# A causal convolution and a routed two-layer network: another order of loads, copies and biases in the head

## The chip, the cores and the metric

The kernel runs on one core of a Trainium2 chip. The metric is device time in microseconds: the median of several executions. One execution was also profiled; its span is the time from the first to the last instruction that the profile shows. The engines are TensorE (PE, with PEld for the weight loads), VectorE (DVE), ScalarE (ACT), GpSimd (POOL) and SyncE (SP, which here only issues DMAs).

## The reference

`x` is 8 x 3584 x 192 in float32. Per head of 24 channels (8 heads) a causal convolution with 7 taps runs along the sequence; the taps are a softmax of `weight`. The rows that come out (28672 of 192) go through a gate, each to one of 8 experts, and through that expert's two layers.

```python
w = softmax(weight)                                  # 8 heads x 7 taps
y = np.einsum('hk,bskhg->bshg', w, x_unf)            # x_unf: the 7 rows up to s
y = y.reshape(N, D)                                  # N = 28672, D = 192
logits = y @ w_gate + modality_bias[modality_id]     # N x 8
e_idx = np.argmax(logits, axis=1)
gate_w = softmax(logits)[np.arange(N), e_idx]
for e in range(E):
    mask = e_idx == e
    h = np.maximum(y[mask] @ w1[e], 0.0)             # 192 -> 1024
    out[mask] = gate_w[mask, None] * (h @ w2[e])     # 1024 -> 192
```

## The kernel before

**The head's unit is a group.** A tile is 112 rows of one batch element. The 256 tiles are dealt out in 19 groups of 4, 4, 8, 8, 8 and then 16 tiles (`QUADS_OF_GROUP`, in quads of four tiles); g0 to g18 below. A block is the same 112 rows of all eight batch elements, 8 tiles; a group of 16 tiles holds two blocks. For each group `Group` does the following, as parts of a generator (`body`) that the main loop advances:

- `load`: x of four tiles per DMA, on SP's queue (384 KB).
- `convolve(h)`: a head is one matmul with a banded matrix, `band` (128 x 112 per head), into a PSUM tile `cv` out of four. Groups below 10 (`WHOLE_X`) multiply in float32, later ones with `band_hi`, `band_lo` and x split in two. The result is copied to the row buffer `y`, by ScalarE for heads with h % 3 < 2 and by VectorE for the others, one copy for each block (L284, L286). There are four `y` buffers (y0 to y3), each for one block; `routed_y` deals them out in turn, one for each block of a group, a group of 4 tiles having one to itself.
- `bias_of`: GpSimd makes the modality bias of the group's tiles in two operations (L293 multiply, L296 add).
- `turn`, `gate`, `logits`, `choose`: a transpose on VectorE, the gate's product, and the argmax with the softmax's denominator. GpSimd writes the row numbers into `y` with an iota (L363).
- `place`: each row's position in its expert's list (`idx`); `send`: one indirect DMA per tile on GpSimd's queue (`scatter`, L212) writes 112 rows into `routed_rows` in HBM.

**The routed steps.** The groups are gathered in chunks; the first chunk has groups 0 to 3 (24 scatters). When a chunk's groups are placed, VectorE makes a table of slots, each a run of rows of one expert. For a slot SP loads w1 (`raw1`, L626 and L628) and w2 (`raw2`, L631), which are split in high and low halves by ScalarE and VectorE (`split`, L100 and L101), and `bring` loads its rows, a lot of two passes of 256 rows at a time: 4 DMAs `near`, 8 DMAs `far` and 1 DMA `tags` (L656). These wait for the chunk's scatters to land. `turn` transposes a pass (`tp`); `first` (L707) and `second` (L727, L731) are the two products in three or two terms, `hh` and `hl` (L710, L711) the halves between them. The finished rows `o` go out by another indirect DMA on GpSimd's queue (L746).

**What sets the order.** Each engine runs its instructions in the order of the program. The main loop (`run`) puts the head's parts between the steps by due times: `marks` and `due` say how many parts are to stand ahead of which step. `AHEAD` parts stand ahead of the first step, `WAIT` empty ones ahead of the last scatters of the first chunk. `tc.issue_after` puts one instruction behind another on its engine. In the head, `warm(n)` gives TensorE n matmuls that nothing reads, so that it is not idle. A `y` buffer is written again only when the scatters that read it have landed, so the copies into it wait on them; the two buffers of a group's two blocks are written head by head in turn, first and second block.

**The filler.** A dummy slot behind the routed rows is filled with a constant tile by 8 DMAs on ScalarE's queue (`make_filler`, L594).

## Time and profile before

| | |
|---|---|
| executions | 1268.9, 1269.66 and 1277.72 us, median 1269.66 us |
| the profiled execution | 1275.32 us |
| its span | 1273.5 us |
| mean granted clock of TensorE in it | 0.985 |
| busy: PE, DVE, ACT, POOL | 96%, 78%, 58%, 42% of the span |
| the chain that ended last | PE 80%, DVE 7%, issue 4%, DMA 3%, POOL 2%, SP's queue 2%, ACT 2% |

The profiled execution is 5.66 us above the median. Busy shares are means over the span, and the stages differ: the head, in which groups are made and no routed step runs, ends near 69 us; up to about 900 us parts of groups stand between the routed steps, after it only routed steps. The granted clock is given as a share of full speed, where 1.00 is 2.4 GHz and 0.50 is 1.2 GHz.

### The profile page before, as it was taken

How to read it: one execution, taken by the hardware profiler on the slowest of the kernel's cores; microseconds unless marked ns; L12 is line 12 of the kernel's file. 1: busy time of each engine (PE TensorE's matmuls, PEld its weight loads, DVE VectorE, ACT ScalarE, POOL GpSimd, SP SyncE). 2: the span in 40 equal slices, each digit the busy share in tenths (PEclk: the TensorE clock that was granted, in tenths of full speed). 3: DMA queues.
4: the chain of work that ended last, by engine and by line, in shares of the span. 5: the costliest groups of instructions: out<-in, count | busy, mean ns of one | idle time of the engine just before them, and what ended most of it. 6: DMA issues, size and time to landing. Idle time of an engine off the chain costs nothing.

```text
span 1273.5 us, 28724 instructions
## 1 busy us (share of the span) xinstructions
PE 1223.5 (96%) x9106; PEld 1189.3 (93%) x9106; DVE 999.1 (78%) x2545; ACT 735.6 (58%) x1644; POOL 538.3 (42%) x574
## 2 busy tenths in 40 slices
PE   9668799999999999999999999999999999999996
PEld 7467689999999999999999999999999999999996
DVE  5669788787888788877888788877877676687895
ACT  2245465565665666656565666556555555566774
POOL 4736655353636343443636344343536222121221
PEclk9889899999999999999999999999999999999998
DMA  6678355324355445426444444333326234496441
GB/s 174 193 164 210 100 137 123 94 72 109 75 134 137 108 103 129 104 61 141 97 115 101 107 100 125 88 84 71 73 54 177 54 78 109 102 253 159 113 108 46
DMA packets 317525, 145.91 MB, mean 115 GB/s; under 512 B 229170, under 2 KB 303531, under 8 KB 317364
## 3 DMA queue, kind: packets, MB, share of 16 engines
q1 hardware_dynamic: 291748, 98.64, 36.3%
q0 software_dynamic: 23232, 44.30, 10.9%
q8 instruction: 73, 1.20, 0.4%
q10 hardware_dynamic: 2384, 1.06, 0.3%
q14 instruction: 88, 0.72, 0.2%
HBM read 118.16 MB, written 51.82 MB: 133 GB/s over the span
## 4 chain that ended last, share of the span: by engine, by line
PE 80%; DVE 7%; issue 4%; DMA 3%; POOL 2%; SPq 2%; ACT 2%; DVEq 0%; POOLq 0%; ACTq 0%
PE hps L707 37%; PE po L727 23%; PE po L731 11%; PE cv L279 5%; PE gt L323 3%; DVE hl L711 1%; DMA routed_rows<-y,idx 1%; SPq L656 1%; POOL routed_rows L212 1%; DVE w1b L101 1%; PE hps L115 1%; DMA xr<-in_x_dram 1%; DVE xl L101 1%; DMA x<-in_x_dram 1%; DVE tp L683 1%
## 5 line engine op out<-in xcount | busy, mean ns | idle before, releaser
L727 PE MATMUL po<-w2b,hh 128*128 128x384 f32 x1824 | 556.3, 355 | 3.5 <-DVE o L745 2.2
L707 PE MATMUL hps<-sxh,w1b 128*128 128x256 f32 x1824 | 486.2, 289 | 11.2 <-ACT sxh L692 8.5
L710 ACT ACTIVATE hh<-hps 128x512 fp32r<-128x512 f32 x456 | 272.5, 598 | 312.6 <-PE hps L707 305.9
L711 DVE SCALAR_TENSOR_TENSOR hl<-hps,hh 128x512 fp32r<-128x512 f32 x456 | 311.3, 685 | 179.6 <-ACT hh L710 176.9
L731 PE MATMUL po<-w2b,hl 128*128 128x192 f32 x1824 | 443.3, 253 | 0.0
L212 POOL DMA_INDIRECT routed_rows<-y,idx x256 | 269.1, 1051 | 334.5 <-DVE hl L711 169.5
L746 POOL DMA_INDIRECT out_dram<-o,tags x228 | 239.4, 1050 | 370.8 <-DVE o L745 299.4
L707 PEld LDWEIGHTS hps<-sxh,w1b 128*128 128x128 f32 x1824 | 345.6, 190 | 21.4 <-DVE hl L711 9.5
L707 PE MATMUL hps<-sxs,w1b 128*128 128x256 f32 x1824 | 364.6, 281 | 0.5 <-DVE sxs L694 0.5
L727 PEld LDWEIGHTS po<-w2b,hh 128*128 128x128 f32 x1824 | 344.3, 189 | 5.1 <-DVE o L745 3.3
L731 PEld LDWEIGHTS po<-w2b,hl 128*128 128x128 f32 x1824 | 346.4, 191 | 0.0
L707 PEld LDWEIGHTS hps<-sxs,w1b 128*128 128x128 f32 x1824 | 280.7, 190 | 0.8 <-DVE sxs L694 0.8
L707 PE MATMUL hps<-sxl,w1b 128*128 128x256 f32 x912 | 257.1, 282 | 0.0
L707 PEld LDWEIGHTS hps<-sxl,w1b 128*128 128x128 f32 x912 | 173.4, 190 | 2.2
L101 DVE TENSOR_TENSOR w1b<-raw,w1b 128x512 fp32r<-128x512 f32 x152 | 101.1, 675 | 4.5 <-ACT w1b L100 4.0
L743 ACT ACTIVATE lowp<-po,tags 128x192 f32<-128x192 f32 x228 | 83.5, 418 | 30.8 <-PE po L727 30.8
L284 ACT COPY y<-cv 112x192 f32<-112x192 f32 (+1 forms) x198 | 53.5, 318 | 79.9 <-PE cv L279 54.6
L101 DVE TENSOR_TENSOR w2b<-raw,w2b 128x384 fp32r<-128x384 f32 x152 | 80.9, 542 | 15.2 <-ACT w2b L100 14.9
L100 ACT CAST w1b<-raw 128x512 fp32r<-128x512 f32 x152 | 92.4, 621 | 0.7
L745 DVE SCALAR_TENSOR_TENSOR o<-po,tags,lowp 128x192 f32<-128x192 f32 x228 | 84.4, 411 | 2.3 <-ACT lowp L743 2.3
L692 ACT CAST sxs<-tp 64x128 fp32r<-64x128 f32 x228 | 67.9, 298 | 30.3 <-DVE tp L685 27.5
L100 ACT CAST w2b<-raw 128x384 fp32r<-128x384 f32 x152 | 76.2, 513 | 3.6 <-DMA raw<-in_moe_w_dram 2.5
(133 smaller groups left out, 1028.5 us busy)
## 6 DMA issues: line engine op xcount, KB each, us to landing
raw<-in_moe_w_dram SPq DMA_DIRECT2D x38, 768.0 KB
raw<-in_moe_w_dram SPq DMA_DIRECT2D x38, 512.0 KB
raw<-in_moe_w_dram SPq DMA_DIRECT2D x76, 256.0 KB
xr<-in_x_dram SPq DMA_DIRECT2D x36, 384.0 KB
near<-routed_rows SPq DMA_DIRECT2D x212, 64.0 KB
x<-in_x_dram SPq DMA_DIRECT2D x26, 384.0 KB
far<-routed_rows SPq DMA_DIRECT2D x456, 16.0 KB
routed_rows<-filler SPq DMA_DIRECT2D x8, 776.0 KB
```

The lines of the kernel that those rows point to most:

```text
L100: nc.scalar.copy(out=hi, in_=raw)
L101: return nc.vector.tensor_tensor(out=lo, in0=raw, in1=f(hi), op=ALU.subtract).ins
L212: state["scatter"] = nc.gpsimd.indirect_dma_start(out=scr, out_offset=bass.IndirectOffsetOnAxis(ap=idx, axis=0), in_=src, in_offset=None,).ins
L692: nc.scalar.copy(out=hi, in_=raw)
L707: nc.tensor.matmul(hps[:, u, :], wa[:, c, fs], mv[z], start=n == 0, stop=n == len(terms) - 1)
L710: nc.scalar.activation(out=hh, in_=hps, func=AF.Relu)
L711: hl_ins = nc.vector.scalar_tensor_tensor(out=hl, in0=hps, scalar=0.0, in1=f(hh), op0=ALU.max, op1=ALU.subtract)
L727: nc.tensor.matmul(po, hh[:, u, js], wb[:, c, :], start=c == 0, stop=c == NF - 1, skip_group_check=True)
L731: nc.tensor.matmul(po[:, 0:D], hl[:, u, js], wb[:, c, 0:D], start=False, stop=False, skip_group_check=True)
L743: nc.scalar.activation(out=lowp, in_=po[:, D:2 * D], func=AF.Copy, scale=gate)
L745: turn_behind(nc.vector.scalar_tensor_tensor(out=o, in0=po[:, 0:D], scalar=gate, in1=lowp, op0=ALU.mult, op1=ALU.add))
L746: st = nc.gpsimd.indirect_dma_start(out=out, out_offset=bass.IndirectOffsetOnAxis(ap=tag.bitcast(I32)[:, j, 1:2], axis=0), in_=o, in_offse ...
```

## The change

1. **x loads.** The x of groups 0 to 4 lies in two buffers (`PACKS`) rather than in one each, in turn, and all its loads are issued at the start; those of groups from 2 on wait for the band's DMA (`behind_band`). The filler is one DMA of all its 776 KB on SP's queue, behind them.
2. **Biases.** Those of the first 48 tiles (g0 to g5) are made in one multiplication and one addition (`first_bias`), before any group; later groups make their own, as before.
3. **Convolutions.** Groups below 10 go by block and in pairs of heads (`convolve_pair`): two matmuls of 192 columns into one PSUM tile and one copy of 384 columns to `y`, by VectorE for each fourth part less two, else by ScalarE. The first block's four pairs come first, then the second's. g0 and g1 share one `y` buffer, and a group of 4 tiles takes its half.
4. **Bands.** `band_hi` and `band_lo` are made at group 8 rather than at the start. `mt` is copied behind the gate's copies on VectorE.
5. **Weights.** w2 of the first slot is asked for behind w1, before the row loads.
6. **Rows.** A lot's `far` rows come in 4 DMAs of 32 KB rather than 8 of 16 KB, so 9 loads a lot rather than 13; the rows of a lot are dealt to its two passes in stripes.
7. **TensorE.** `WARM2` = 20 more warm matmuls stand ahead of the first routed step, and the first convolutions of groups 2 to 4 stand behind an earlier group's gate (`GATED`).

```diff
+BEFORE_BAND = 2
+GATED = {2: 1, 3: 1, 4: 2}
+PACKS = (0, 4, 8), (0, 8)
...
-WARM2 = 0
+WARM2 = 20
...
-        nc.sync.dma_start(out=band, in_=bass.AP(lines.tensor, 0, [[1, P], [wide, H], [1, MB]]))
+        state["band"] = nc.sync.dma_start(out=band, in_=bass.AP(lines.tensor, 0, [[1, P], [wide, H], [1, MB]])).ins
...
-        split(hi, lo, band)
...
-        nc.vector.tensor_copy(out=mt.rearrange("p b s -> p (b s)"), in_=mt_ps)
+        with tc.issue_after(state["wg"]):
+            nc.vector.tensor_copy(out=mt.rearrange("p b s -> p (b s)"), in_=mt_ps)
...
-    def routed_y():
-        turns["y"] = turns.get("y", -1) + 1
+    def routed_y(fresh):
+        turns["y"] = turns.get("y", -1) + fresh
...
+    def make_bias(dst, n, ids):
+        nb = ids.shape[1]
+        nc.gpsimd.tensor_tensor(
+            out=dst.rearrange("p (s b) e -> p s b e", s=n), in0=ids.rearrange("p b s -> p s b").unsqueeze(3).broadcast_to([MB, n, nb, E]),
+            in1=step.unsqueeze(1).unsqueeze(1).broadcast_to([MB, n, nb, E]), op=ALU.mult)
+        nc.gpsimd.tensor_tensor(out=dst, in0=dst, in1=start_row.unsqueeze(1).broadcast_to([MB, n * nb, E]), op=ALU.add)
+
+    def behind_band(ins):
+        tc.add_manual_dep(ins, state["band"].name, mybir.DependencyInfo(
+            mybir.DependencyClass.Sync, mybir.DependencyReason.DATA), reason="the bands come first")
...
+            packed = sum(len(p) for p in PACKS)
+            pack = sum(g >= sum(len(p) for p in PACKS[:i]) for i in range(1, len(PACKS))) if g < packed else len(PACKS) + g - packed
+            at = ([i for p in PACKS for i in p] + [0] * NG)[g]
...
-                self.x = xp.tile([P, NT, D], F32, name="x", tag=self.place_x)
+                if at == 0:
+                    turns["x"] = xp.tile([P, NT, D], F32, name="x", tag=self.place_x)
+                self.x = turns["x"][:, at:at + 4 * QUADS_OF_GROUP[g], :]
...
+        def load(self, q, after_band=False):
+
+            with tc.issue_after(state["x"]) if self.g >= sum(len(p) for p in PACKS) else nullcontext():
+                self.load_behind(q, after_band)
...
+            if after_band:
+                behind_band(ld.ins)
...
+        def convolve(self, part):
+
+            if part == 0:
+                self.ys = [routed_y(self.b0 == 0) for _ in range(self.blocks)]
+            if self.whole_x:
+                with tc.issue_after(state["gates", GATED[self.g]]) if self.g in GATED and part == 0 else nullcontext():
+                    self.convolve_pair(part)
+                return
+            h = part
...
+        def convolve_pair(self, part):
+            i, h = divmod(2 * part, H)
+            if i >= self.blocks:
+                return
+            cv = ring(ps_t, 4, [MB, 2, self.nb, G], F32, "cv", "t")
+            for k in range(2):
+                hs = slice((h + k) * G, (h + k + 1) * G)
+                nc.tensor.matmul(cv[:, k], band[:, h + k, :], self.x[:, i * NB:i * NB + self.nb, hs], start=True, stop=True)
+            dst = self.ys[i][0:MB, self.b0:self.b0 + self.nb, OVER + h * G:OVER + (h + 2) * G].rearrange("p b (k c) -> p k b c", k=2)
+            if part % 4 != 2:
+                nc.scalar.copy(out=dst, in_=cv)
+            else:
+                nc.vector.tensor_copy(out=dst, in_=cv)
...
+            if self.g < len(AT_ONCE):
+                self.bt = first_bias[:, AT_ONCE[self.g]:AT_ONCE[self.g] + self.tiles]
+            else:
+                self.bt = rt.tile([MB, NT, E], F32, name="bt")[:, 0:self.tiles]
+                make_bias(self.bt, n, mt[:, self.b0:self.b0 + self.nb, self.block:self.block + n])
...
+        early = []
+        for g in range(sum(len(p) for p in PACKS)):
+            early.append(Group(g, chunk_of[g]))
+            for q in range(early[-1].quads):
+                early[-1].load(q, g >= BEFORE_BAND)
+        with tc.issue_after(state["x"]):
+            ins = nc.sync.dma_start(out=scr[DUMMY:DUMMY + TW, :].rearrange("(j p) w -> p j w", p=P),
+                                    in_=filler.unsqueeze(1).broadcast_to([P, TW // P, W])).ins
+        tc.add_to_no_dep_group("rows0", ins)
+        scatters.append((0, ins.name))
+        cur, ends = early[0], iter(())
...
+            if g == WHOLE_X - 2:
+                split(band_hi, band_lo, band)
...
-        for j in range(TW // P):
-            ins = nc.scalar.dma_start(out=scr[DUMMY + j * P:DUMMY + (j + 1) * P, :], in_=dr).ins
-            tc.add_to_no_dep_group("rows0", ins)
-            scatters.append((0, ins.name))
...
-            if i > 0:
-                load_second()
+            load_second()
...
-            squares = src.rearrange("(k j s t) w -> k j t s w", j=NJ, s=P // Q, t=Q)
-            parts += [(far[j * DB + q * Q:j * DB + (q + 1) * Q, k - k0], squares[k, j, :, :, OVER + P + q * Q:OVER + P + (q + 1) * Q])
-                      for k in range(k0, k1) for j in range(NJ) for q in range(DB // Q)]
+            each = squares.shape[1] // NJ
+            parts += [(far[j * DB + q * Q:j * DB + (q + 1) * Q].rearrange("p k s c -> p (k s) c"),
+                       squares[:, j * each:(j + 1) * each, OVER + P + q * Q:OVER + P + (q + 1) * Q])
+                      for j in range(NJ) for q in range(DB // Q)]
...
-            if self.i == lot == 0:
-                with tc.issue_after(ld):
-                    self.load_second()
...
+    first_bias = const.tile([MB, 6 * NB, E], F32, name="first_bias")
+    make_bias(first_bias, 6, mt[:, :, 0:6])
```

GpSimd's queue between the last scatter of g1 and the scatters of g4, of before (`y_219` is g2's buffer, `y_220` g3's):

```order
L363 IOTA y_219 112x8
L293 TENSOR_TENSOR bt<-mt,step 112x64
L296 TENSOR_TENSOR bt<-bt,both 112x64
L212 DMA routed_rows<-y_219,idx 238592x194 x8
L363 IOTA y_220 112x8
L293 TENSOR_TENSOR bt<-mt,step 112x128 x2
L296 TENSOR_TENSOR bt<-bt,both 112x128 x2
L212 DMA routed_rows<-y_220,idx 238592x194 x8
L363 IOTA y_217 112x8
L212 DMA routed_rows<-y_217,idx 238592x194 x8
```

and of after (`y_218` is g2's, `y_219` g3's, `y_220` g4's):

```order
L405 IOTA y_218 112x8
L215 DMA routed_rows<-y_218,idx 238592x194 x8
L405 IOTA y_219 112x8
L215 DMA routed_rows<-y_219,idx 238592x194 x8
L405 IOTA y_220 112x8
L215 DMA routed_rows<-y_220,idx 238592x194 x8
```

The bias operations between the scatters are gone; what is left between them is the iota.

ScalarE's copies of g7, the group whose buffers are read by g5's scatters, of before (`y1` belongs to the first block, `y2` to the second; the last scatters out of `y2` are the latest):

```order
L284 COPY y1_218<-cv_1696 112x8x24
L284 COPY y2_219<-cv_1696 112x8x24
L284 COPY y1_218<-cv_1700 112x8x24
L284 COPY y2_219<-cv_1700 112x8x24
L100 CAST w2b0_91<-raw2_0_87 128x2x192
L692 CAST sxh_1733<-tp_1730 128x256
L692 CAST sxs_1735<-tp_1730 64x128 x2
L710 ACTIVATE hh_1753<-hps_1742 128x512
L284 COPY y1_218<-cv_1768 112x8x24
L284 COPY y2_219<-cv_1768 112x8x24
```

and of after (here the first block is `y0`, the second `y1`):

```order
L328 COPY y0_217<-cv_1653 112x2x8x24
L328 COPY y0_217<-cv_1657 112x2x8x24
L103 CAST w2b0_91<-raw2_0_87 128x2x192
L737 CAST sxh_1690<-tp_1687 128x256
L737 CAST sxs_1692<-tp_1687 64x128 x2
L755 ACTIVATE hh_1710<-hps_1699 128x512
L328 COPY y0_217<-cv_1725 112x2x8x24
L328 COPY y1_218<-cv_1730 112x2x8x24
L328 COPY y1_218<-cv_1735 112x2x8x24
```

The first copy into the second block's buffer stood second; it is now the eighth row, behind a cast of w2, three casts of rows, one `hh` step and three copies into the first block's buffer.

SP's queue around the first row loads, of before (`raw_0_85` is w1, `raw_0_87` w2 of the first slot):

```order
L656 DMA far<-routed_rows 32x4x32
L656 ISA
L656 DMA far<-routed_rows 32x4x32
L656 ISA
L656 DMA tags<-routed_rows 128x4x2
L631 ISA
L631 DMA raw_0_87<-in_moe_w_dram 128x8x192
```

and of after:

```order
L676 DMA raw_0_85<-in_moe_w_dram 64x1024
L679 ISA
L679 DMA raw_0_87<-in_moe_w_dram 128x8x192
L689 TENSOR_LOAD tab
L689 ISA x2
L704 ISA
L704 DMA near<-routed_rows 32x16x32
```

The request for w2 stood behind the last row load; now it stands ahead of the first, and ahead of the register load that begins the row loads.

## Rows read from the trace of the kernel before

**Rows 1.** Windows by stage: busy time of each engine, granted clock, DMA share.

```profile
core 0: us, PE busy (x) PEld busy (x) DVE busy (x) ACT busy (x) POOL busy (x), PEclk, DMA share, GB/s
60.00:80.00 20.00, 8.60 (x40) 7.07 (x38) 9.47 (x18) 6.37 (x14) 4.75 (x6) 0.74 0.61 147
100.00:120.00 20.00, 16.54 (x114) 14.85 (x115) 18.70 (x40) 11.22 (x24) 13.07 (x12) 1.00 0.84 227
120.00:140.00 20.00, 14.37 (x79) 11.29 (x78) 13.12 (x55) 7.38 (x21) 11.29 (x14) 0.83 0.58 152
300.00:1180.00 880.00, 879.22 (x6740) 875.24 (x6739) 696.03 (x1706) 526.13 (x1154) 360.47 (x366) 1.00 0.46 108
```

**Rows 2.** Timeline of POOL, 26 to 66 us.

```profile
36.99 0.94 POOL L212 DMA_INDIRECT routed_rows<-y,idx  x1 [0.30 <-issue]
...
40.66 0.97 POOL L212 DMA_INDIRECT routed_rows<-y,idx  x1 [1.86 <-issue]
...
50.59 0.81 POOL L293 TENSOR_TENSOR bt<-mt,step 112x128 f32<-112x128 f32 x2
51.36 0.86 POOL L296 TENSOR_TENSOR bt<-bt,both 112x128 f32<-112x128 f32 x2
...
61.13 0.94 POOL L212 DMA_INDIRECT routed_rows<-y,idx  x1 [0.30 <-issue]
```

**Rows 3.** Chain of waits, 60 to 82 us: start, duration, what.

```profile
61.13 2.44 DMA routed_rows<-y,idx
```

**Rows 4.** Waits of the SP queue, 40 to 80 us: total, times, longest, us.

```profile
SPq L656 <- DMA routed_rows<-y,idx: 10.4, 3, 8.0
```

**Rows 5.** Timeline of ACT, 50 to 80 us; idle time before in brackets.

```profile
52.58 0.54 ACT L284 COPY y<-cv 112x192 f32<-112x192 f32 x2 [7.37 <-DMA routed_rows<-y,idx]
...
76.27 1.75 ACT L100 CAST w2b<-raw 128x384 fp32r<-128x384 f32 x4 [2.51 <-DMA raw<-in_moe_w_dram]
```

**Rows 6.** Timeline of ACT around 94 and 133 us.

```profile
94.77 0.76 ACT L284 COPY y<-cv 112x192 f32<-112x192 f32 x3 [1.35 <-DMA routed_rows<-y,idx]
...
133.11 0.76 ACT L284 COPY y<-cv 112x192 f32<-112x192 f32 x3 [8.66 <-DMA routed_rows<-y,idx]
```

**Rows 7.** Timeline of PE, 124 to 145 us.

```profile
133.48 3.68 PE L279 MATMUL cv<-x,band 128*112 128x384 f32 x6 [5.63 <-ACT y L284]
```

**Rows 8.** Chain of waits, 100 to 140 us.

```profile
100.60 2.17 PE cv L279 x6
...
127.47 5.41 DMA routed_rows<-y,idx
...
137.17 1.18 PE hps L707 x10
```

**Rows 9.** Timeline of ACT, 13 to 18 us.

```profile
14.25 0.94 ACT L100 CAST band_hi<-band 128x896 fp32r<-128x896 f32 x1 [6.32 <-DMA band<-tap_lines]
14.25 2.29 ACTq L594 DMA_DIRECT2D routed_rows<-filler  x5
16.59 0.52 ACT L284 COPY y<-cv 112x96 f32<-112x96 f32 x3 [1.41 <-DMA routed_rows<-filler]
```

**Rows 10.** Copies into tile y: duration ns min/median/max, first and last start, forms.

```profile
L284 ACT COPY y<-cv x198: 238/322/357, 16.6 to 895.2; 112x192 f32<-112x192 f32 x186, 112x96 f32<-112x96 f32 x12
L286 DVE COPY y<-cv x66: 257/347/359, 16.6 to 889.9; 112x192 f32<-112x192 f32 x62, 112x96 f32<-112x96 f32 x4
```

**Rows 11.** Timeline of the SP queue, 58 to 78 us.

```profile
66.03 4.38 SPq L656 DMA_DIRECT2D far<-routed_rows  x8
...
71.28 0.40 SPq L631 DMA_DIRECT2D raw<-in_moe_w_dram  x1
```

**Rows 12.** Window of 130 to 135 us, columns as in rows 1.

```profile
130.00:135.00 5.00, 1.52 (x3) 0.86 (x4) 1.30 (x7) 1.86 (x7) 0.99 (x1) 0.50 0.87 283
```

**Rows 13.** Timeline of POOL, 100 to 140 us.

```profile
103.27 0.95 POOL L212 DMA_INDIRECT routed_rows<-y,idx  x1 [7.05 <-ACT y L284]
...
127.47 0.97 POOL L212 DMA_INDIRECT routed_rows<-y,idx  x1 [0.26 <-DVE pos L386]
```

More of the change, by code (lines that the diff above doesn't have):

```diff
@@ L179, in make_gate @@
             nc.vector.tensor_copy(out=whole[rows, :, q * Q:q * Q + E], in_=wg[rows])
-            nc.vector.tensor_copy(out=parts[rows, :, q * Q:q * Q + 2 * E], in_=f(wgs[rows]))
+            state["wg"] = nc.vector.tensor_copy(out=parts[rows, :, q * Q:q * Q + 2 * E], in_=f(wgs[rows])).ins
         return whole, parts
@@ L267, in part @@
             split(self.xh[:, part, :], self.xl[:, part, :], self.xr[q])
-        def convolve(self, h):
-            if h == 0:
-                self.ys = [routed_y() for _ in range(self.blocks)]
+        def convolve(self, part):
[6 more added lines that the diff above has]
+            h = part
             cv = ring(ps_t, 4, [MB, self.tiles, G], F32, "cv", "t")
             hs = slice(h * G, (h + 1) * G)
-            if self.whole_x:
-                terms = ((band, self.x[:, 0:self.tiles, :]),)
-            else:
-                terms = (band_hi, self.xh), (band_hi, self.xl), (band_lo, self.xh)
+            terms = (band_hi, self.xh), (band_hi, self.xl), (band_lo, self.xh)
             for n, (wt, xt) in enumerate(terms):
@@ L397, in send @@
             for t in range(t0, t1):
-                scatter(self.chunk, self.idx[:, t:t + 1], self.ys[t // NB][0:MB, t % NB, :])
+                scatter(self.chunk, self.idx[:, t:t + 1], self.ys[t // NB][0:MB, self.b0 + t % NB, :])
     chunk_of = [c for c, n in enumerate(GROUPS_OF_CHUNK) for _ in range(n)]
     FIRST = GROUPS_OF_CHUNK[0]
+    AT_ONCE = [4 * sum(QUADS_OF_GROUP[:g]) for g in range(NG) if sum(QUADS_OF_GROUP[:g + 1]) <= 12]
     def parts_of(g):
@@ L415, in body @@
     def body(cur, after):
-        if after:
+        if after and not after.xr:
             for q in range(min(3, after.quads)):
@@ L429, in body @@
                 yield
-            if t == 0 and after and after.whole_x and after.quads > 3:
+            if t == 0 and after and after.whole_x and after.quads > 3 and len(after.xr) == 3:
                 after.load(3)
@@ L452, in all_groups @@
     def all_groups():
-        cur, ends = Group(0, 0), iter(())
-        for q in range(cur.quads):
-            cur.load(q)
-            cur.part(q)
+        early = []
[9 more added lines that the diff above has]
+        cur, ends = early[0], iter(())
         for g in range(NG):
-            after = Group(g + 1, chunk_of[g + 1]) if g + 1 < NG else None
+            if g == WHOLE_X - 2:
+                split(band_hi, band_lo, band)
+            after = (early[g + 1:g + 2] or [Group(g + 1, chunk_of[g + 1])])[0] if g + 1 < NG else None
             done, tiles = 0, 4 * QUADS_OF_GROUP[g - 1]
@@ L682, in turn @@
             with tc.issue_after(state["o"]) if "o" in state else nullcontext():
-                nc.vector.transpose(out=tp[:, 0:NJ].rearrange("p j (s t) -> p (j s) t", t=Q),
-                                    in_=self.rows[lot][:, k0 * T // Q:(k0 + 1) * T // Q])
+                nc.vector.transpose(out=tp[:, 0:NJ].rearrange("p j (s t) -> p j s t", t=Q),
+                                    in_=self.rows[lot].rearrange("p (j k s) t -> p j k s t", j=NJ, s=P // Q)[:, :, k0])
                 nc.vector.transpose(out=tp[:, NJ].rearrange("p (s t) -> p s t", t=Q), in_=self.ends[lot][:, k0])
@@ L695, in turn @@
             self.h["x", k] = [z.rearrange("p j s -> p (j s)") for z in (xh, xl, xs)]
[L696 removed]
+            self.h["tag", k] = self.tags[lot].rearrange("p (j k) o -> p j k o", j=NJ)[:, :, k0]
             state["vector"] = turned
```

36 lines of the change are left out of this document (15 added, 21 removed).

## The prediction

> **What bounds the kernel now.** I read the windows by stage first. In the long stretch from 300 to 1180 us TensorE is busy for 879.22 of 880 us at a granted clock of 1.00 [rows 1]. Nothing that the change does to other engines can shorten that stretch, and its amount of TensorE work stays as it is; what is left to win lies in front of it, where TensorE stands idle: 11.4 us between 60 and 80, 3.5 between 100 and 120, 5.6 between 120 and 140 [rows 1]. The last steps after 1240 us wait too, but no edit touches them. Since TensorE never rests after 180 us, each microsecond by which the routed steps start earlier, or by which a stall in the head gets shorter, should come off the end, unless another wait takes its place.
>
> Then I followed what holds the first routed step. The chain is POOL's row of scatters: the first four groups have 24, one every 1.25 us, the last from 61.13 [rows 2], and it lands 2.44 us later [rows 3]; only then may SP ask for the rows, for which its queue has waited 8.0 us [rows 4]. Behind that ScalarE waits 2.51 us more for w2 [rows 5]. Last I looked for the long stall. At 133 us ScalarE has waited 8.66 us for scatters to leave a y buffer [rows 6], TensorE 5.63 us for ScalarE [rows 7], and the chain of waits names the scatter issued at 127.47, which took 5.41 us to land [rows 8].
>
> **The change, part by part.** All sums are made against the profiled execution: 1275.32 us, span 1273.5. That lies 5.66 above the median of the three runs, 1269.66; I carry the same 5.66 off at the end.
>
> *A. Up to the last scatter of the first four groups.* ScalarE issues five filler DMAs at once, 2.29 us long, behind the cast of band_hi; the first eviction starts at 16.59 after 1.41 us of that wait [rows 9]. With the filler on SP and the band split moved to group 8, the eviction can start when the first convolution is there, a little after 14.4: 2.1 us sooner. In groups 0 and 1 a pair of heads leaves PSUM in one copy of 192 columns instead of two of 96. From the fastest copy (96 columns, 0.238) and the median (192 columns, 0.322) [rows 10], three copies at 0.32 take the place of six at 0.24, some 0.5 us in the chain of a group. So the indices of group 2 come 2.6 us sooner. POOL can follow, since between the end of group 1's last scatter (36.99 + 0.94 = 37.93) and the first of group 2 (40.66) it has 2.7 us without a scatter [rows 2]. Between groups 2 and 3 it makes four bias operations, 0.81 and 0.86 us in two pairs, from 50.59 to 52.2 [rows 2]; these go, leaving the iota, so 1.45 us go. Together -4.0. The bound on the small side counts POOL's bias work ahead of group 3 alone: -1.5. The large side lets group 2's scatters follow group 1's with no gap but the iota, all moved by 2.1: -5.9. The one large bias pair of 112x384 at the start has no row; two 112x128 take 0.81 together [rows 2], so I put it at 0.6 to 1.2 us an operation, and it runs while VectorE makes the indices of group 0, for which POOL has to wait. That wait is its cover; without it up to 2.4 us would be late.
>
> *B. w2 sooner.* ScalarE's wait of 2.51 us ahead of w2's cast [rows 5] is for a request issued at 71.28, behind thirteen row loads [rows 11]. It now stands ahead of the row loads, before SP's wait for the scatters, and lands with w1. Of the 2.51 us I take 1.9, because TensorE at its low clock needs part of that time for the first products anyway; bounds 0 and -2.5. Nothing that is late stands behind it on SP's queue: the first row load waits for the scatters for 8.0 us there [rows 4].
>
> Against this stands what a scatter does under load. The last scatter of the first chunk lands in 2.44 us [rows 3], the one at 127.47 in 5.41 [rows 8], while the DMA share rises to 0.87 [rows 12]. If w2 and the x loads that now come earlier were still moving, the first row loads would start 3.0 us later, and A to D would come to 3.0 less. *The Trainium skill* says so on the page "DMA: Bandwidth & Descriptors", section "Latency and other measured facts": an access to HBM takes 0.2 us on average and 2 us at high load, and with a lighter load a DMA's fixed cost falls. By that rule the last scatter would land up to 1.8 us later (an estimate from that page), so that the sum would be smaller by it; the two rows above agree in direction, with a difference of 3.0. I don't take it as likeliest: w2 is requested ahead of that wait of 8.0 us [rows 4], and the request at 71.28 had landed by 76.27 [rows 5, 11], thus in under 5 us.
>
> *C. The y buffers by block.* In before a copy of y1 and a copy of y2 alternate on ScalarE, head by head, so that the first head's second copy needs all scatters of the buffer that is freed last. In after the four pairs of the first block are written first; ScalarE's first row on the second buffer is the eighth of the group's stretch, no longer the second. Until it blocks TensorE, TensorE now has five more pairs of convolutions, at 0.36 (six in 2.17), and two more steps of the routed products, each 2.3 (ten products of the first kind take 1.18, the second kind about as much) [rows 8]: 1.8 + 4.6 = 6.4 us. The stall of 5.63 us [rows 7] lies under that, with little to spare. The copies by ScalarE and the indices of group 6 on VectorE, behind the wait before, are ahead of it now, so POOL's next scatters come sooner too. The granted clock is 0.50 in the five microseconds that follow the stall [rows 12]: six convolutions there take 3.68 us [rows 7], at 100 us they took 2.17 [rows 8], so 1.5 us go with the stall. I take -7.1. Bounds: -2.4 if half the stall stays and the clock still falls in it (2.8, less 0.4 for waits moved elsewhere), -8.7 if all that ScalarE lost, 8.66, comes back. What comes next is POOL: from 103.27 to 127.47 [rows 13] it issues 18 DMAs and a pair of bias operations, 1.34 us to a DMA, and the change leaves them there.
>
> *D. Work on VectorE between 80 and 160.* VectorE is busy 18.70 of 20 us there [rows 1]. A copy of 192 columns costs it 0.347 [rows 10]; of a group of 16 tiles it has some five, after two of 384 columns at an estimated 0.5 (the slope from 96 to 192 columns, 0.09, twice on top). This is 0.87 us a group and three groups lie here: -2.6. The band split, moved in from the head, adds one subtraction of 128x896; ScalarE's cast of that size took 0.94 [rows 9], so I put it at 1.1. With 0.4 for the wait of 1.35 at 94.77 [rows 6]: -1.9, bounds 0 and -4 (no gain at all, or both halves without the split and the wait gone whole).
>
> *E. At nothing.* The pairs cost TensorE the same number of columns, two of 192 for one of 384. The twenty warm matmuls run in idle time between the last head convolutions and the first rows; cover: 8 us and more of idle TensorE, as ScalarE's wait of 7.37 us at 52.58 [rows 5] goes too. They end about 10 us before the first rows, too soon, I think, to hold the clock. Nine row loads instead of thirteen save SP four issues of 0.55 us [rows 11], not on the path, as the first pass needs four near and four far loads either way. x loads behind the band: the band is there when the first convolution starts, and x of group 0 and 1 still goes first.
>
> Sum: -4.0 - 1.9 - 7.1 - 1.9 = -14.9, so 1260.4 for such an execution, 1254.8 for the median.
>
> **The rivals.** *R1, the stall stays.* POOL's stream bounds the second buffer as before: the 18 DMAs at 1.34 us each end just as late against TensorE's work, and ScalarE stands at a later row but as long. For it: POOL has next to no free time from 103.27 to 127.47 [rows 13], and the landing of 5.41 us [rows 8] comes on top. Against: the 6.4 us of new cover. Price: C is lost, -7.8 is left, 1261.9 for the median.
>
> *R2, traffic.* The last scatter of the first chunk lands like the one at 127.47, +3.0 as above: median 1257.8.
>
> *R3, slower.* A far load now holds 32 KB, both passes of a lot. The first pass can't start before all four are there, where before it needed the first four of eight, 2.2 us at 0.55 an issue [rows 11]; if an issue takes time by its bytes, each lot is ready 2.2 us later. It decides if lots come later than their lead: from seven late lots the gain is gone, ten make it +7.1, median 1276.8. Against it: TensorE waits 0.8 us in 880 [rows 1], so lots come with a lead now.
>
> *R4, the warm matmuls hold the clock.* I have put them at nothing; if they reach the first rows, the clock is up there. The granted clock of 60 to 80 is 0.74 [rows 1], and 8.6 us of TensorE work are done there, half of it slow; at full clock 2.2 us go: median 1252.6.
>
> **How the numbers follow.** Forecast as summed 0.52, R1 0.20, R2 0.15, R3 0.05, R4 0.08. The predicted time is that of the forecast, 1254.8. Its own range from the nearer bounds of A to D is 1249 to 1262; the range has to reach R1 with its spread and the far end of R4: 1248 to 1265, leaving out R3, the far tails and some of R1. About one per cent, 1256.96, is what a measurement of this kernel tells from no change. The forecast lies under it by little: 0.33 of its 0.52 is faster, with 0.07 of R4, 0.06 of R2 and 0.03 of R1 0.49; slower is R3 and a tail, 0.06; the rest, 0.45, is within.
>
> **What would show it.** A: the last scatter of the fourth group from about 57 instead of 61.13. B: no wait of ScalarE for w2. C: no idle time of TensorE over 2 us between 110 and 140, and a clock of 1.00 there. D: VectorE's copies of 384 columns at about 0.5. Between 300 and 1180 TensorE busy as now; if it isn't, R3. Wrong would be the prediction by a new wait that I don't see: x of group 5 or 6 late, since x loads now stand behind the band, or a pair's copy that holds a PSUM bank longer than two heads did.

## The result, and the profile after

The changed kernel takes 1260.38 us (median of 6, 1258.32 to 1263.09); the kernel before, run beside it again, 1272.61 (median of 6). The ratio is 0.990, interval 0.9881 to 0.992: 12.2 us less (10.2 to 15.1), against 14.9 forecast. The profiled execution took 1259.42 us with a span of 1257.7, 15.8 less than the span of before; it lies 1.0 under its median, that of before 2.7 over its new one, so the two traces show some 3.7 us more than the medians.

The windows by stage, of after; the columns are those of rows 1.

```profile
60.00:80.00 20.00, 14.27 (x86) 12.97 (x86) 12.69 (x26) 8.78 (x18) 5.70 (x5) 0.76 0.76 153
80.00:100.00 20.00, 18.65 (x133) 17.82 (x134) 19.55 (x50) 13.78 (x31) 7.37 (x9) 1.00 1.00 262
100.00:120.00 20.00, 18.13 (x132) 17.23 (x132) 18.66 (x54) 11.46 (x26) 15.77 (x17) 1.00 0.82 214
120.00:140.00 20.00, 17.34 (x127) 16.44 (x125) 19.36 (x52) 12.17 (x24) 15.57 (x18) 1.00 0.21 64
300.00:1180.00 880.00, 878.73 (x6736) 874.41 (x6735) 698.64 (x1715) 528.81 (x1157) 356.67 (x363) 1.00 0.46 108
```

Nothing moved between 300 and 1180, as forecast. Between 100 and 140 TensorE's idle time fell from 9.1 to 4.5 us, and the granted clock stays at 1.00 there [rows 1]. From 60 to 80 it fell from 11.4 to 5.7.

The way to the first product, of after: POOL from 20 to 60 us, the chain of waits behind its last scatter, SP's queue, then TensorE and ScalarE.

```profile
22.94 1.12 POOL L215 DMA_INDIRECT routed_rows<-y,idx  x1 [5.48 <-DVE ad L418]
...
35.33 0.94 POOL L215 DMA_INDIRECT routed_rows<-y,idx  x1 [2.24 <-DVE lt L372]
...
51.80 2.43 POOL L215 DMA_INDIRECT routed_rows<-y,idx  x1 [0.30 <-issue]
...
55.78 0.94 POOL L215 DMA_INDIRECT routed_rows<-y,idx  x1 [0.30 <-issue]
```

```profile
55.78 2.46 DMA routed_rows<-y,idx
```

```profile
46.75 0.40 SPq L679 DMA_DIRECT2D raw<-in_moe_w_dram  x1
58.45 2.08 SPq L704 DMA_DIRECT2D near<-routed_rows  x4
```

```profile
64.03 0.79 PE L752 MATMUL hps<-sxh,w1b 128*128 128x256 f32 x2 [8.28 <-ACT sxh L737]
```

```profile
13.78 0.66 ACT L328 COPY y<-cv 112x192 f32<-112x192 f32 x2 [6.95 <-PE cv L325]
...
68.61 1.75 ACT L103 CAST w2b<-raw 128x384 fp32r<-128x384 f32 x4
```

The first copy starts at 13.78 instead of 16.59 [rows 9], the scatters of group 2 at 35.33 instead of 40.66, the last of the first chunk at 55.78 instead of 61.13 [rows 2]. It lands in 2.46 us, as before in 2.44 [rows 3], although w2 is asked for at 46.75; the rows are asked for at 58.45, 2.67 us after that scatter's issue. ScalarE casts w2 at 68.61 with no wait, where it waited 2.51 us at 76.27 [rows 5].

How far ahead the changed kernel is at each point can be read from `hh`, which ScalarE makes 456 times, in the same order in both kernels. The first, second, 14th and 22nd, of before and then of after:

```profile
73.17 0.60 ACT L710 ACTIVATE hh<-hps 128x512 fp32r<-128x512 f32 x1 [2.27 <-PE hps L707]
78.67 0.58 ACT L710 ACTIVATE hh<-hps 128x512 fp32r<-128x512 f32 x1
...
122.81 0.59 ACT L710 ACTIVATE hh<-hps 128x512 fp32r<-128x512 f32 x1
...
160.44 0.59 ACT L710 ACTIVATE hh<-hps 128x512 fp32r<-128x512 f32 x1
```

```profile
67.99 0.60 ACT L755 ACTIVATE hh<-hps 128x512 fp32r<-128x512 f32 x1 [2.27 <-PE hps L752]
71.00 0.59 ACT L755 ACTIVATE hh<-hps 128x512 fp32r<-128x512 f32 x1
...
113.75 0.59 ACT L755 ACTIVATE hh<-hps 128x512 fp32r<-128x512 f32 x1
...
144.65 0.59 ACT L755 ACTIVATE hh<-hps 128x512 fp32r<-128x512 f32 x1
```

The lead is 5.2 us at the first, 7.7 at the second (the cast of w2 stands between), 9.1 at the 14th and 15.8 at the 22nd, behind the place of the long stall. It is 17.3 at the 30th and 15.8 in the spans; what moves it there is not settled.

### The profile page after: what moved, and what is told of

It reads as the page before. It is cut to its first block, busy times and chain, and to the rows that moved or that the text cites. A ratio compares the mean times of both kernels' runs of the same rounds, so it can differ in the third digit from the quotient of the medians.

```text
span 1257.7 us, 28099 instructions
## 1 busy us (share of the span) xinstructions
PE 1221.8 (97%) x9206; PEld 1201.2 (96%) x9206; DVE 999.1 (79%) x2530; ACT 732.6 (58%) x1599; POOL 538.9 (43%) x564
## 4 chain that ended last, share of the span: by engine, by line
PE 84%; DVE 7%; DMA 3%; issue 3%; ACT 1%; POOL 1%; SPq 1%; DVEq 0%; POOLq 0%; ACTq 0%
PE hps L752 38%; PE po L772 24%; PE po L776 11%; PE gt L365 4%; PE cv L309 3%; PE cv L325 2%; DVE hl L756 1%; DMA xr<-in_x_dram 1%; PE hps L118 1%; POOL routed_rows L215 1%; DVE w1b L104 1%; DVE xl L104 1%; DVE gx L104 1%; DMA raw<-in_moe_w_dram 1%; ACT lowp L788 1%
## 5 line engine op out<-in xcount | busy, mean ns | idle before, releaser
L739 DVE TENSOR_TENSOR sxs<-tp,sxs 64x128 fp32r<-64x128 f32 x228 | 65.9, 289 | 9.0 <-ACT sxs L737 0.4
```

## The experiments

The first four ran on one chip, beside the kernel before at 1273.33 us; the changed kernel did not run beside them, so they are set against the 0.990 above. The others ran on two more chips, on which the kernel before took 1298.15 us (e12_filler, e3, e11, e5) and 1299.52 us (e13, e12_filler_again, e7, e8). Ratios are to the kernel before on the same chip. On the third chip the changed kernel ran too and comes out at 1.0002; so expectations that name 0.990 don't hold for these, and kernels of one chip are set against each other. "The first chip" below is that of the first four; whether the runs of before and after above were on the same chip isn't known, but the times of before are alike (1272.61 and 1273.33 us).

### The blocks in turn again (e1_alternate)

```diff
-            i, h = divmod(2 * part, H)
-            if i >= self.blocks:
+            part, i = divmod(part, self.blocks)
+            h = 2 * part
+            if h >= H:
                 return
```

> The changed kernel with the pairs of a two-block group written in turn, first block, second block, as before; all else stays. Theory (the order of the blocks hides the wait for the scatters of the later buffer): ScalarE waits 4 to 8 us for scatters again near 120 to 130 us, TensorE stands idle 4 to 6 us behind it at the lower clock, and the time is 5 to 7 us above the changed kernel, about 0.995 of the kernel before. Rival (the stall went because copies are fewer and POOL is earlier, the order matters nothing): no wait of TensorE over 2 us there, 0.990 of the kernel before as the change itself.

Measured: 1269.08 us, 0.9958 (0.9944 to 0.9972), so 0.0058 or 7.4 us above the changed kernel. ScalarE and TensorE of this run, around the stall:

```profile
123.83 0.86 ACT L329 COPY y<-cv 112x384 f32<-112x384 f32 x2 [6.61 <-DMA routed_rows<-y,idx]
```

```profile
124.36 2.90 PE L326 MATMUL cv<-x,band 128*112 128x192 f32 x8 [3.23 <-ACT y L329]
```

```profile
120.00:140.00 20.00, 16.12 (x94) 15.26 (x92) 13.85 (x38) 10.72 (x24) 12.92 (x16) 0.83 0.22 69
```

ScalarE's wait is back with 6.61 us, TensorE's with 3.23, and the clock in the window is 0.83 as before [rows 1]. The window's idle time, 3.9 us, is not all of it; the low clock adds its part, and ScalarE waits in front of copies into `y` for 3.42 us at 87.78 and 3.19 at 157.22 too. Against the changed kernel the 14th `hh` comes 1.4 us later (115.11) and the 22nd 7.0 (151.60). The theory holds in its mechanism, with a shorter wait of TensorE than the 4 to 6 us expected; the rival falls.

### The order of the blocks alone (e10_before_blocks)

In the kernel before, two-block groups in float32 go block by block, two heads to a PSUM tile; copies stay one head wide.

```diff
+            if self.whole_x and self.blocks == 2:
+                i, h = divmod(2 * h, H)
+                cv = ring(ps_t, 4, [MB, 2, self.nb, G], F32, "cv", "t")
+                for k in range(2):
+                    hs = slice((h + k) * G, (h + k + 1) * G)
+                    nc.tensor.matmul(cv[:, k], band[:, h + k, :], self.x[:, i * NB:i * NB + self.nb, hs], start=True, stop=True)
...
+                return
```

> The kernel before with the one edit that two-block groups in float32 are convolved block by block, two heads at a time (copies stay one head wide, as many as before). Theory: the stall at 133 us (TensorE 5.63 idle) goes, and the time falls by some 7 us, 0.9945 of before. Rival (the stall goes only together with the earlier scatters and the fewer copies): it falls by under 2 us, 0.9985 or more.

Measured: 1285.44 us, 1.0085 (1.0064 to 1.0106): 11 us slower. Neither theory said so. TensorE's stall is gone as forecast; its longest waits between 110 and 145 us are 1.2 us, this one and one of 1.18 at 141.35:

```profile
118.17 0.44 PE L739 MATMUL po<-w2b,hh 128*128 128x384 f32 x1 [1.19 <-DVE o L757]
```

But the head is later. VectorE and POOL of this run, at the scatters of group 2:

```profile
43.53 0.36 DVE L282 COPY y<-cv 112x192 f32<-112x192 f32 x1 [3.85 <-DMA routed_rows<-y,idx]
43.80 0.16 DVE L402 CAST idx<-row 112x8 int32<-112x8 f32 x1
```

```profile
44.76 0.97 POOL L212 DMA_INDIRECT routed_rows<-y,idx  x1 [5.67 <-ACT y L280]
```

The copies of group 5's first block go into y1, which group 1's scatters still read; here they stand ahead of the cast of group 2's indices on VectorE, wait there 3.85 us, and group 2's scatters start at 44.76 instead of 40.66 [rows 2]. By `hh` the run is 5.7 us behind the kernel before at the first (78.83) and 9.6 at the 14th (132.41), of which these 4.1 us are a part. From the 14th to the 22nd it takes 32.4 us instead of 37.6: there the order of the blocks gives 5.2 back, as the theory said. The first loss is larger, and some 6 us more are lost later, most of it between 225 and 300 us; why isn't shown. So the order of the blocks takes one wait away and puts another ahead of the first rows, unless the rest of the change (g0 and g1 in one buffer, other buffers for g5, the convolutions behind an earlier gate) keeps it off. Which of these does so wasn't tried.

### w2 behind the row loads again (e2_w2_late)

```diff
-            load_second()
+            if i > 0:
+                load_second()
...
             state["load"] = ld
+            if self.i == lot == 0:
+                with tc.issue_after(ld):
+                    self.load_second()
```

> The changed kernel with the first slot's w2 asked for behind the first lot's row loads again. Theory (w2 was on the path): ScalarE waits some 2 us for it ahead of its cast, and all that follows is 1.9 to 2.5 us later, 0.992 of the kernel before. Rival (VectorE's queue bounds the steps behind it, so w2's moment is hidden): 0.990, as the change.

Measured: 1259.83 us, 0.9881 (0.9858 to 0.9903): no slower than the changed kernel as far as these times can tell. SP's queue and ScalarE of this run:

```profile
61.23 2.32 SPq L705 DMA_DIRECT2D far<-routed_rows  x4
...
64.47 0.39 SPq L679 DMA_DIRECT2D raw<-in_moe_w_dram  x1
```

```profile
69.42 1.75 ACT L103 CAST w2b<-raw 128x384 fp32r<-128x384 f32 x4 [0.34 <-DMA raw<-in_moe_w_dram]
```

The rival on time holds, but not for its reason: the wait itself is nearly gone, 0.34 us, with w2 behind the rows. From the first far load to the request for w2 it is 3.24 us here (61.23 to 64.47); it was 5.25 in before (66.03 to 71.28), where eight far loads took 4.38 [rows 11] and not four 2.32. That loses 0.3 us between the first and the second `hh`, the 0.34 of the wait.

### Filler and band split at the start again (e4_filler_split)

The eight filler DMAs are on ScalarE's queue in `make_filler` again and SP's one is gone; `split(hi, lo, band)` is back in `make_bands`.

```diff
+        split(hi, lo, band)
...
-            if g == WHOLE_X - 2:
-                split(band_hi, band_lo, band)
...
+        for j in range(TW // P):
+            ins = nc.scalar.dma_start(out=scr[DUMMY + j * P:DUMMY + (j + 1) * P, :], in_=dr).ins
```

> The changed kernel with the filler as eight DMAs on ScalarE's queue and the band split at the start again. Theory (the first copies were held by these): first scatter some 2 us later than 22.94, last scatter of the first chunk 2 to 3 us later than 55.78, time 1 to 3 us above the changed kernel, as VectorE gets one subtraction less later: 0.991 to 0.9925 of before. Rival (POOL's gap ahead of group 2's scatters takes it up): last scatter within 0.5 us of 55.78, and 0.990 or a little less.

Measured: 1267.4 us, 0.9949 (0.9934 to 0.9965), so 0.0049 or 6.2 us above the changed kernel. ScalarE and POOL of this run:

```profile
10.94 0.94 ACT L103 CAST band_hi<-band 128x896 fp32r<-128x896 f32 x1 [4.43 <-DMA routed_rows<-filler]
10.94 5.93 ACTq L640 DMA_DIRECT2D routed_rows<-filler  x7
16.91 0.76 ACT L329 COPY y<-cv 112x192 f32<-112x192 f32 x3 [5.04 <-DMA routed_rows<-filler]
```

```profile
26.62 1.12 POOL L216 DMA_INDIRECT routed_rows<-y,idx  x1 [8.44 <-ACT y L329]
```

```profile
60.44 0.94 POOL L216 DMA_INDIRECT routed_rows<-y,idx  x1 [0.30 <-issue]
```

SP's queue of this run, the request for w2 and the first rows:

```profile
57.66 0.39 SPq L677 DMA_DIRECT2D raw<-in_moe_w_dram  x1
66.10 1.94 SPq L702 DMA_DIRECT2D near<-routed_rows  x4
```

The filler holds the first copy to 16.91, the first scatter goes at 26.62 (22.94 in the changed kernel), the last at 60.44 (55.78). The mechanism of the theory is right, its size was not: 4.7 us at the last scatter, not 2 to 3, and 6.2 us of time, not 1 to 3. More is lost behind the last scatter. w2 is asked for 2.8 us ahead of it here, not 9.0; the DMAs move 266 to 358 GB/s from 58 to 64 us, and the rows are asked for 5.66 us after its issue, not 2.67. That is 3.0 more, as rival R2 of the prediction has it. The first `hh` comes 7.45 us later (75.44). The profiled execution, 1270.61 us, is the longest of seven; how often this happens in the others isn't shown.

### The filler alone, on other chips (e12_filler, e12_filler_again)

> The changed kernel with the filler as eight DMAs on ScalarE's queue again, but with the band split still at group 8. With both put back the time was some 6 us above the changed kernel, with ScalarE held 4.4 and 5.0 us behind filler DMAs. Theory (the filler on ScalarE's queue holds the first copies, the split is cheap): nearly all of it comes back, first scatter 3 us or more later than 22.94, 0.9945 to 0.996 of the kernel before. Rival (the two full-width band operations in the head cost as much as the filler): half of it, 0.992 to 0.993.

> The changed kernel with the filler as eight DMAs on ScalarE's queue, the band split at group 8, once more beside the changed kernel. Theory (the filler on ScalarE's queue holds the first copies, and that is what the head gained): first scatter 3 us or more later, time 4 to 7 us above the changed kernel. Rival (the split at the start is as much of it): 2 to 3 us above.

Only the filler's part of the edit above. Measured: 1.0013 (0.9995 to 1.0031) on the second chip and 1.0012 (0.9998 to 1.0025) on the third. The first scatter goes at 27.51 and 25.69. On the third the changed kernel stands beside it at 1.0002, so no difference can be told there. How filler and split share the 6.2 us is left open.

### The changed kernel on another chip (e13_after)

> The changed kernel as it is, so that the three beside it have it on the same chip. 0.990 of the kernel before, as measured first; if the chip is one on which all kernels are 2% longer, the ratio shows whether the change is worth the same there.

Measured: 1302.06 us beside 1299.52, 1.0002 (0.998 to 1.0024). The change is worth nothing there. Part of the reason is in VectorE's timeline: the first and the last operation shown of the first slots' table, of the changed kernel on the first chip, then of the same kernel here.

```profile
38.89 0.15 DVE L572 TENSOR_TENSOR cnt<-carry,base 1x8 f32<-1x8 f32 x1
...
42.84 0.14 DVE L625 TENSOR_TENSOR tab<-past,live 1x4 int32<-1x4 f32 x1
```

```profile
45.32 0.15 DVE L572 TENSOR_TENSOR cnt<-carry,base 1x8 f32<-1x8 f32 x1
...
57.24 0.17 DVE L619 TENSOR_REDUCE srow<-of 1x4 f32<-1x32 f32 x1 [2.48 <-remote]
...
60.74 0.15 DVE L625 TENSOR_TENSOR tab<-past,live 1x4 int32<-1x4 f32 x1 [1.18 <-DVE ad L418]
```

The same operations take 4.1 us there and 15.6 here. Most of these operations take no longer than on the first chip; between them VectorE stands still, the longest times for "remote" (2.48 and 1.76 us ahead of L619 and L622), once for "issue" (1.27 us), that is, for nothing that the profile shows, and in part behind an operation of its own. TensorE's waits from 0 to 180 us have the same:

```profile
PE cv L325 <- issue: 8.2, 2, 6.9
PE hps L118 <- remote: 6.3, 1, 6.3
PE po L772 <- issue: 4.8, 5, 1.8
PE gt L365 <- issue: 3.9, 3, 3.3
```

In the traces of before and after from the first runs TensorE has no such wait in these 180 us. SP's queue and POOL of this run:

```profile
59.79 0.94 POOL L215 DMA_INDIRECT routed_rows<-y,idx  x1 [0.30 <-issue]
```

```profile
64.40 0.38 SPq L674 DMA_DIRECT2D raw<-in_moe_w_dram  x1
...
68.21 5.09 SPq L704 DMA_DIRECT2D near<-routed_rows  x4
```

The last scatter goes at 59.79, but the table is done at 60.9, so w1 is asked for at 64.40 and the first rows at 68.21. SP waits for the table and not for the scatters. Here the table bounds the first rows, not POOL's row; earlier scatters are then worth nothing. That is 13.9 us at the first `hh` (81.87 for 67.99); another 21.5 us are lost by the 22nd (180.00). The kernel before was timed there but not profiled, so where it spends its 27 us more isn't shown.

### Thirteen row loads, and w2 behind them (e3_thirteen, e11_thirteen_late)

The first puts back eight far loads of 16 KB a lot, with the transposes that go with them; the second does that and puts w2 behind, as in e2_w2_late.

```diff
-            parts += [(far[j * DB + q * Q:j * DB + (q + 1) * Q].rearrange("p k s c -> p (k s) c"),
-                       squares[:, j * each:(j + 1) * each, OVER + P + q * Q:OVER + P + (q + 1) * Q])
-                      for j in range(NJ) for q in range(DB // Q)]
+            parts += [(far[j * DB + q * Q:j * DB + (q + 1) * Q, k - k0], squares[k, j, :, :, OVER + P + q * Q:OVER + P + (q + 1) * Q])
+                      for k in range(k0, k1) for j in range(NJ) for q in range(DB // Q)]
```

> The changed kernel with thirteen row loads a lot (8 far of 16 KB), w2 still asked for ahead of them. Theory (the four issues saved lie beside other work): 0.990 of the kernel before, within 0.002, first product at 64.0 as now. Rival (bigger far loads come later and cost lead): faster than the changed kernel, 0.988 or less; second rival (SP's queue is on the path behind the first lot, where the next slot's w1 and w2 and the next lot wait for it): 2 us or more slower, 0.992 or more.

> Thirteen row loads and w2 behind them, as both were before; all else of the change stays. With w2 behind nine loads nothing was lost. Theory (the nine loads and the early w2 do the same thing twice, each alone takes the wait for w2 away): ScalarE waits 2 us or more for w2 and the time is 2 us above the changed kernel, 0.9915 to 0.993. Rival (w2's moment never mattered, since VectorE bounds the steps behind): within 0.001 of the run with thirteen loads and early w2.

Measured, both on the second chip: 1.0021 (1.0006 to 1.0036) and 1.0004 (0.9982 to 1.0027). The expected ratios were meant for the first chip; only the two runs can be set against each other, and their times don't differ. ScalarE's first cast of w2, of e3_thirteen and then of e11_thirteen_late:

```profile
81.09 1.76 ACT L103 CAST w2b<-raw 128x384 fp32r<-128x384 f32 x4
```

```profile
81.86 1.75 ACT L103 CAST w2b<-raw 128x384 fp32r<-128x384 f32 x4 [2.79 <-DMA raw<-in_moe_w_dram]
```

With thirteen loads and w2 behind them the wait is there (2.79 us); with either undone it isn't (here, and 0.34 us in e2_w2_late on the first chip). So the two edits do take the same wait away twice. From the first to the second `hh` it is 5.8 us with the wait and 3.0 without; that this costs time in the end was not shown on this chip.

### The biases by group (e5_bias_each)

```diff
-            if self.g < len(AT_ONCE):
+            if self.g < 0:
...
-    make_bias(first_bias, 6, mt[:, :, 0:6])
```

> The changed kernel with each group's bias made by itself again, in POOL's row. Theory (POOL's row of scatters sets the first rows): two bias pairs of 112x128 stand between the scatters of groups 2 and 3 again, the last scatter leaves 1.4 to 1.9 us later than 55.78, time 1.5 us above the changed kernel, 0.991. Rival (hidden, as w2 was): 0.990 or less.

Measured on the second chip: 0.9954 (0.9933 to 0.9975), faster than all others there. Its table takes from 43.85 to 51.69, and SP's first near load goes at 64.03, behind the last scatter at 59.19. There the scatters set the first rows again, not the table as in e13_after, and the first product goes at 69.19 us, against 76.16 in e3_thirteen on the same chip. w2 is asked for at 58.43 here, 0.8 us ahead of the last scatter, and the rows 4.84 us after it: as in e4_filler_split. The bias work itself can't make that out, and why the table came through sooner isn't shown. So with the biases by group the change is worth 6 us there; the changed kernel itself didn't run on that chip. What the biases cost on the first chip wasn't measured.

### More warm matmuls (e7_warm45)

```diff
-WARM2 = 20
+WARM2 = 45
```

> The changed kernel with 45 warm matmuls ahead of the first routed step, the added 25 all behind the last but one pair of group 4. Theory (the twenty end too soon to hold the clock): the added ones fill some 6 to 10 us of TensorE's 8.3 us of idle time ahead of the first product, the granted clock there is 1.00 instead of 0.50, and 2 us go: 0.998 of the changed kernel. Rival (at the lower clock they take 0.42 us each, 10 us, and push the first product out): 2 us above it. Second rival: nothing, since VectorE bounds the steps behind, 80 to 140 us.

Measured on the third chip: 0.9996 (0.9983 to 1.0008) beside 1.0002 (0.998 to 1.0024). TensorE and ScalarE up to the first product, and the window of the first products, of this run; then ScalarE's cast and the same window of e13_after:

```profile
72.35 6.04 PE L118 MATMUL hps<-ones 112*112 112x448 bf16 x29
...
79.40 0.53 PE L752 MATMUL hps<-sxh,w1b 128*128 128x256 f32 x2
```

```profile
78.65 0.41 ACT L737 CAST sxh<-tp 128x256 fp32r<-128x256 f32 x1 [3.22 <-issue]
```

```profile
80.00:85.00 5.00, 3.26 (x26) 2.86 (x25) 2.62 (x7) 2.93 (x8) 0.77 (x1) 1.00 0.76 219
```

```profile
77.17 0.41 ACT L737 CAST sxh<-tp 128x256 fp32r<-128x256 f32 x1 [3.26 <-DVE tp L728]
```

```profile
80.00:85.00 5.00, 5.00 (x22) 4.79 (x23) 2.50 (x5) 3.11 (x7) 1.01 (x1) 0.50 0.96 238
```

The clock is held: 1.00 instead of 0.50 at the first products, with 29 warm matmuls in a row and eight convolutions behind them where TensorE of e13_after stood idle for 5.47 us. From the first product to the first `hh` it is 3.24 us, not 4.24, so 1.0 us is gained there. The first product goes 1.8 us later than in e13_after (79.40, 77.63), but its rows are later too: ScalarE's cast of them starts 1.5 us later, and this run was 2.0 us behind already at TensorE's convolutions ahead of all added matmuls (56.97 for 54.97). At most 0.3 us is the matmuls' own price. The time is the same within its interval; the first theory has its mechanism and half of its 2 us, in one trace.

### All copies of groups 5 to 9 on ScalarE (e8_act_copies)

```diff
-            if part % 4 != 2:
+            if part % 4 != 2 or self.g > FIRST:
```

> The changed kernel with all copies of convolutions of groups 5 to 9 on ScalarE, none on VectorE. Theory (after the change VectorE bounds the stretch from 80 to 140 us, busy 57.6 of 60 us, ScalarE 37.4): VectorE loses 8 to 10 copies of 0.5 us, TensorE's idle time of 5.9 us there falls by 2 to 3, 0.998 of the changed kernel. Rival (ScalarE's queue stands behind scatters in these copies, and VectorE's are then later too): 0 to 3 us slower.

Measured on the third chip: 0.9989 (0.9968 to 1.001) beside 1.0002 (0.998 to 1.0024): the intervals overlap. From 80 to 140 us VectorE is busy 43.97 us here and 43.87 in e13_after, far from the 57.6 of the first chip, so there it isn't the bound that this run was to relieve. Inconclusive.

## Why the prediction was right, and where it wasn't

The time lies in the range, and the sign and the likeliest case were right where before and after were first compared: 12.2 us of 14.9. The interval of the 12.2, 10.2 to 15.1 us, holds the 14.9, so the times alone don't show a term to be too large. The traces, 15.8 us apart, let each be set against its stretch: 5.2 up to the first `hh` (A, 4.0 forecast), 2.5 from there to the second (B, 1.9), 1.4 to the 14th (D, 1.9), 6.7 to the 22nd (C, 7.1; its first steps touch D too).

**A, up to the last scatter.** Right in its mechanism, mis-sized: 5.35 us instead of 4.0 at the last scatter, inside the bounds, and e4_filler_split gives back 4.7 of them. The two halves came out otherwise: group 2's scatters are 5.3 us earlier (35.33 for 40.66), twice the 2.6 that I took from the first copy and the smaller ones; the 1.45 us of bias work between groups 2 and 3 are gone, but one scatter, at 51.80, takes 2.43 us instead of 0.94 and uses them up; that the two halves still come near the sum is luck.

**B, w2 sooner.** The wait of 2.51 us is gone, and nearly all of it came off: 2.5 us between the first and the second `hh`, not the 1.9 left over for TensorE's low clock. The step that failed is whose gain it is. It was booked for the moved request, but moving the request back costs 0.3 us in the trace and nothing that the times can tell (e2_w2_late), because four far loads instead of eight bring it 2.0 us ahead anyway. Those loads I had put at nothing in E, since the first pass needs as many either way; I overlooked that w2 stands behind them. Each edit alone takes the wait away.

**R2, traffic.** It doesn't show in the changed kernel: the last scatter landed in 2.46 us, since w2, asked for 9.0 us ahead of it, had passed by then (DMA share 0.15 from 54 to 56 us). It does show in e4_filler_split, where w2 is asked for 2.8 us ahead of the last scatter and the rows follow that scatter 3.0 us later than in the changed kernel, and in e5_bias_each. This agrees in direction with the Trainium skill, page "DMA: Bandwidth & Descriptors", section "Latency and other measured facts", by which HBM answers more slowly at high load; it is more than the 1.8 us estimated from that page. So the early w2 may have a use that the prediction didn't give it, to keep the load away from the last scatters; no run moved it by itself to show that.

**C, blocks in order.** Right: 7.1 forecast, 7.4 shown by undoing it; no wait of TensorE from 80 to 160 us is longer than 1.1, and its clock is 1.00 there. R1 falls. But I had treated it as an edit by itself, and by itself it is 11 us slower (e10_before_blocks): it gives 5.2 back at the stall, but the first block's copies then wait ahead of the first chunk's indices.

**D, VectorE from 80 to 160.** Mis-sized, by a wrong count. Of a group's sixteen copies VectorE had four in before (66 of 264 in all [rows 10]), not some five. Two copies of 384 columns at 0.547 (the median of VectorE's copies into `y`; ScalarE's is 0.482) for four at 0.347 save 0.29 us a group, 0.9 in three groups and not 2.6; the band split takes 1.22, near the 1.1 put in, but starts only at 147.6 us. By these numbers D comes to about -0.1. Still 1.4 us are gained between the second and the 14th `hh`. Apart from the long stall, TensorE's waits from 80 to 160 us add up to 8.9 us in before and 6.4 after; those that VectorE ended went from 5.6 to 4.8, those for ScalarE's cast of `gx` from 3.3 to 1.6. So what was gained there came in larger part past VectorE's copies, and from which edit isn't shown. After the change VectorE is busy 57.6 of the 60 us from 80 to 140 (19.55, 18.66 and 19.36), with TensorE idle 5.9 there; that VectorE is the bound now is argued from this, as no run on the first chip took the copies off it.

**E and the other rivals.** R3 didn't come: TensorE is busy 878.73 of 880 us from 300 to 1180 with far loads of 32 KB. R4 didn't: the twenty warm matmuls end at 53.2, 10.8 us ahead of 64.03, TensorE stands idle for the last 8.28 us of these, and the clock is 0.50 from 60 to 65 us; e7_warm45 shows that it could be held at 1.00, for about 1 us up to the first `hh` in its trace and no difference in time. The x loads in two buffers, the later copy of `mt` and the convolutions behind a gate were not undone by any run.

What I had no rival for is the last point: that the table could take longer than the scatters. On the third chip it does, and the change is worth nothing there; on the second it does in e12_filler and e3_thirteen but not in e5_bias_each, and the changed kernel itself didn't run.

## What to carry to other kernels

Before an edit is given a price for a wait, list what stands ahead of the waited-for request on its queue; another edit of the same change may already take the wait away, and then the two prices must not be added. An order of writes that spares one buffer's wait moves the first wait to the other buffer: look for what stands behind that on each engine. Where several chains run side by side to one point (here the scatters, the table and w2, all ahead of the first rows), a gain on the longest is worth only its lead over the second, and that lead can differ from chip to chip. Where weights were asked for shortly ahead of the last scatters, the rows behind them came 3.0 us later here: look at what else is in flight when a chain ends in a DMA.

## What the runs showed of the hardware that was not expected

One kernel, the changed one, took 1260.38 us on one chip and 1302.06 on another, and the kernel before 1272.61 and 1299.52. In the trace of the slower chip the large operations last as long as on the other (a product into `po` 0.355 and 0.356 us on average), and from 300 to 1180 us TensorE is nearly as busy (873.09 us, 878.73 on the first). The larger part of the difference lies in the first 180 us (35.4 us at the 22nd `hh`), where the engines stand still between instructions for nothing that the profile shows: TensorE's waits there add up to 25.4 us of "issue" and "remote", none on the first chip. What they wait for isn't settled by these traces.

A single scatter can take 2.43 us on GpSimd instead of 0.94, with the same 0.30 us ahead of it as the others (51.80 in the changed kernel); what holds it isn't shown either.

With weights in flight beside the last scatters the rows behind them came later: 5.66 us after the last scatter's issue with w2 asked for 2.8 us ahead of it (e4_filler_split), 2.67 with 9.0 (the changed kernel).
